# PSUM as one tile of eight banks, handed out singly, and inverse 2 copied bank by bank

## The chip, the cores and the metric

The kernel runs on one core of one Trainium2 chip. The metric is the device time of one execution in microseconds (us); of several executions the median counts. Engines are called as in the profile: PE (TensorE, matrix products into PSUM), DVE (VectorE), ACT (ScalarE), POOL (GpSimd) and SP (SyncE, which issues most DMAs here). PSUM is the memory that PE writes its results to; in this kernel it is 128 partitions by eight banks of 512 fp32 numbers.

## The reference

Two branches work on an input of 2048 positions by 640 channels, and a gate mixes them.

```python
g = sigmoid((u * gate_w).sum(-1, keepdims=True))
K = 2.0 * einsum("dn,dnl->dl", C, P).real          # P = exp(A*dt*pos), 640 channels x 128 states
y = irfft(rfft(u_t, 2*L) * rfft(K, 2*L))[:, :, :L]   # a long convolution per channel
a = y.transpose + u * D_skip
b = relu(x @ w1) @ w2                                # 640 -> 1728 -> 640
out = g * a + (1 - g) * b
```

Gate, convolution and feed-forward all take the same input: `x` is `A_u` (`u` in the convolution), so `B_x` is not used.

## The kernel before

**Feed-forward.** `feed_forward` splits the 1728 hidden units in three passes (`PARTS` 5, 5, 4 blocks of 128). Each fp32 operand is split into a high and a low part, and three products make one: in the profile `xx` holds the inputs (high and low), `w1h`, `w1l`, `w2h`, `w2l` the weights, `hh`, `hl` the hidden values (later passes keep some of these in other tiles' places, so that `w1h` or `w2h` also appear as moving operands). A group of the first product is 15 matmuls of 512 columns into one bank (`hidden`, L393; `wide`, L456); ACT takes the relu of it and DVE the low part. A group of the second product (`sums`, L496) is up to 15 matmuls of 320 columns into one bank, and DVE adds it to the running sum `q`. `trans` (L336) turns the inputs on PE in the first pass. The tiles in PSUM are called pf.

**Generation of the taps.** `ssm` (L854) makes the convolution's taps K out of 128 states, 16 channels at a time: `products` (L911; PSUM tile pg, four banks) and `taps` (L990; pk, one bank). The gate's matmuls use pg too (`spread_gate`, L611), and a tile pe of one bank takes the first matmuls of the program (`spin`, L602).

**Convolution.** `conv` (L1044) works on five blocks of 128 channels. Per block: stage 1 (`stage1`, L1097) multiplies the taps (`ck`) and the inputs (`xu`) by a table `tf`, four steps of four matmuls for each, into two banks; DVE turns each result with two stream transposes into `ku`. Of a result of the taps each transpose reads one bank; of a result of the inputs each reads half of both banks. Stage 2 (`stage2`, L1138; table `tm`) has eight steps of 16 matmuls into two banks: ACT copies one half of both banks to `ku`, DVE multiplies the other half of both with that copy, once into `kx` and once into `ku`, and POOL adds and subtracts. Inverse 2 (`inv2`, L1178; table `tn`) has two halves of 64 matmuls into four banks, which ACT copies out in two copies of two banks. DVE relays them (`relay`), and inverse 1 (`inv1`, L1216; table `tw`) has two steps of four matmuls into two banks, which ACT scales by the gate. The PSUM tiles of the convolution are called pc. They come from a pool of three tiles of two adjacent banks (L1058), opened when the generation's pool (pg, pe, pk; L863) is closed; pf has a pool of two single banks throughout (L229).

**Order.** Nothing is scheduled at run time. Each step is a task in a queue of its engine (`PE.ff`, `PE.s2`, `DVE.su`, ...). The string `ORDER` names a queue by a letter at each place, and `Plan.run` takes the next task from it; what is recorded in that order is each engine's program order. So feed-forward matmuls stand between those of the generation, and later between those of the convolution. `Ring` and `Token` count the buffers: a task takes tokens and others use them, and `run` only asserts that a buffer is free. Where one engine needs another's result, or a buffer that another still reads, the framework that records the kernel adds a semaphore wait, by the regions of tiles that each instruction reads and writes. In inverse 2 the first half's matmuls stand in `PE.s2` behind the eighth step of stage 2 (`LATE` = 4), its copies in `ACT.s2`. All instructions are recorded by one helper, so every row of the profile has its line, L186 (L188 after the change): one goes by the tiles' names.

## Time and profile before

| what | us |
|---|---|
| three runs | 622.92, 621.34, 622.42; median 622.42 |
| the profiled execution, its own time | 621.33 |
| its span in the trace | 619.5 |
| busy in the span: PE, DVE, ACT, POOL | 605.9, 505.9, 376.1, 83.9 |
| mean granted clock of PE | 0.997 |

A row of a group reads: line, engine, operation, the tile written `<-` the tiles read, shapes, count, then busy us and mean ns of one, then the idle us of the engine just before these instructions and what ended most of it. A row of the waits reads: engine, tile and line of the waiting instruction `<-` what released it, then us, count and the longest. A row of the timeline begins with the time from the start of the span and the duration; a number in square brackets is the idle time ahead of it and its releaser.

### The profile page before, as it was taken

The page shows a single profiled execution, that of the slowest core. Times are in us where ns is not written, and L with a number is a line of the kernel's source. Part 1 is how long each engine was busy: PE and PEld are TensorE (multiplying, and loading weights), DVE is VectorE, ACT ScalarE, POOL GpSimd, SP SyncE. Part 2 cuts the span into 40 slices and gives each one's busy share as a digit, 9 for nine tenths or more (in the row PEclk, how much of TensorE's full clock was granted, in tenths as well). Part 3 has the DMA queues.
Part 4 walks back from the last instruction along what each step waited for, and adds up shares of the span by engine and source line. Part 5 has one row for each costly group of instructions (what it writes and reads, how often), then busy time and mean ns, then how long its engine had stood idle before and what let it go on. Part 6 is the DMA issues. An engine that isn't in the chain of part 4 may idle for free.

```text
span 619.5 us, 19956 instructions
## 1 busy us (share of the span) xinstructions
PE 605.9 (98%) x8676; PEld 492.8 (80%) x8676; DVE 505.9 (82%) x841; ACT 376.1 (61%) x539; POOL 83.9 (14%) x114
## 2 busy tenths in 40 slices
PE   7999999999999999999999999999999999999997
PEld 6999998889987898898898888676646755667666
DVE  3798966899999999999999966887859768968642
ACT  3654438999999998899989821313351453432561
POOL 0000000000000000000000000024250360731735
PEclk8999999999999999999999999999999999999999
DMA  9783666135246535453643338982526766664276
GB/s 232 199 321 93 213 218 221 42 81 163 82 134 216 189 138 185 162 170 82 212 165 137 111 116 259 280 247 84 110 75 226 179 156 197 151 168 158 67 200 184
DMA packets 75457, 102.56 MB, mean 166 GB/s; under 512 B 7529, under 2 KB 58601, under 8 KB 75114
## 3 DMA queue, kind: packets, MB, share of 16 engines
q1 hardware_dynamic: 74970, 100.39, 53.8%
q8 instruction: 68, 1.11, 0.8%
q10 hardware_dynamic: 400, 0.90, 0.5%
q14 instruction: 19, 0.16, 0.1%
HBM read 62.21 MB, written 39.06 MB: 163 GB/s over the span
## 4 chain that ended last, share of the span: by engine, by line
PE 76%; ACT 8%; DVE 7%; DMA 4%; issue 2%; SPq 1%; POOL 1%; ACTq 0%; DVEq 0%; POOLq 0%
PE pf L186 51%; PE pc L186 15%; PE pk L186 6%; PE pg L186 4%; ACT sc L186 4%; DVE ku L186 3%; ACT L186 2%; SPq L186 1%; ACT mg L186 1%; DMA xu<-in_A_u_dram 1%; DMA ck<-kd 1%; DVE sc L186 1%; DVE mg L186 1%; DVE G L186 1%; DMA out_dram<-yo 1%
## 5 line engine op out<-in xcount | busy, mean ns | idle before, releaser
L186 PE MATMUL pf<-xx,w1h 128*128 128x256 f32 (+1 forms) x760 | 187.0, 344 | 0.0
L186 PEld LDWEIGHTS pf<-xx,w1h 128*128 128x128 f32 x760 | 124.9, 192 | 28.0 <-issue 13.4
L186 POOL TENSOR_TENSOR ku<-ku,kx 128x256 f32<-128x256 f32 x80 | 56.7, 738 | 473.5 <-DVE ku L186 438.3
L186 PE MATMUL pf<-xx,w1l 128*128 128x512 f32 (+1 forms) x340 | 115.9, 341 | 0.0
L186 ACT COPY ku<-pc 128x512 f32<-128x512 f32 (+1 forms) x60 | 43.7, 753 | 100.4 <-PE pc L186 89.1
L186 PE MATMUL pf<-w2h,hh 128*128 128x320 f32 x288 | 91.4, 322 | 0.3 <-DVE q L186 0.3
L186 DVE STREAM_TRANSPOSE ku<-pc 128x512 f32<-128x512 f32 x80 | 76.8, 1063 | 17.3 <-PE pc L186 17.3
L186 PE MATMUL pf<-w2l,hh 128*128 128x320 f32 x288 | 87.7, 308 | 0.0
L186 PE MATMUL pf<-w2h,hl 128*128 128x320 f32 x256 | 73.7, 313 | 0.0
L186 PEld LDWEIGHTS pf<-xx,w1l 128*128 128x128 f32 x340 | 64.9, 191 | 7.5
L186 PEld LDWEIGHTS pf<-w2h,hh 128*128 128x128 f32 x288 | 54.0, 188 | 11.1 <-issue 5.3
L186 ACT ACT_TABLE_LOAD x42 | 53.9, 1283 | 1.7 <-DVE sc L186 1.0
L186 PEld LDWEIGHTS pf<-w2l,hh 128*128 128x128 f32 x288 | 54.1, 188 | 0.2
L186 DVE TENSOR_TENSOR mg<-mg,sc 128x1024 f32<-128x1024 f32 x40 | 49.0, 1224 | 3.5 <-DVE G L186 0.5
L186 ACT COPY sc<-pg 128x1024 f32<-128x1024 f32 x40 | 40.4, 1010 | 14.7 <-PE pg L186 14.6
L186 DVE TENSOR_TENSOR sc<-sc,mg 128x1024 f32<-128x1024 f32 x40 | 48.6, 1216 | 0.0
L186 PEld LDWEIGHTS pf<-w2h,hl 128*128 128x128 f32 x256 | 46.4, 188 | 2.0 <-issue 1.2
L186 ACT ACTIVATE sc<-sc,half_pi 128x1024 f32<-128x1024 f32 x40 | 45.6, 1140 | 0.0
L186 ACT ACTIVATE hh<-pf 128x512 fp32r<-128x512 f32 (+1 forms) x40 | 20.4, 510 | 36.5 <-PE pf L186 36.5
L186 ACT ACTIVATE sc<-sc 128x1024 f32<-128x1024 f32 x40 | 42.2, 1054 | 0.2
L186 ACT ACTIVATE mg<-pg 128x1024 f32<-128x1024 f32 x40 | 41.7, 1043 | 0.2
L186 PE MATMUL pc<-ku,tm 64*32 64x256 f32 x1280 | 39.8, 379 | 0.6 <-DVE ku L186 0.5
(171 smaller groups left out, 1127.3 us busy)
## 6 DMA issues: line engine op xcount, KB each, us to landing
xx<-xt SPq DMA_DIRECT2D x24, 640.0 KB, 6.5
xt<-xx SPq DMA_DIRECT2D x16, 640.0 KB, 5.0
part<-q SPq DMA_DIRECT2D x16, 640.0 KB, 4.7
q<-part SPq DMA_DIRECT2D x16, 640.0 KB, 4.6
ws<-in_B_w_dram SPq DMA_DIRECT2D x20, 320.0 KB, 3.4
kd<-kt SPq DMA_DIRECT2D x80, 64.0 KB, 3.1
ck<-kd SPq DMA_DIRECT2D x40, 128.0 KB, 3.4
xu<-in_A_u_dram SPq DMA_DIRECT2D x10, 512.0 KB, 8.4
```

Of the source, the lines that this page charges most:

```text
L186: return lambda *a, **k: self._tc.keep_in_program_order(f(*a, **k))
```

## The change

PSUM becomes one tile `ps` of eight banks that lives throughout, and one ring `bk` hands out its banks. A `Ring` now keeps a list of free numbers; `run` gives a token the first of the list, and puts the number at its end when the last user is done. Feed-forward groups, turns of the inputs, `taps`, `spin` take one token each; `products` works in banks 0 to 3, which four tokens (`hold`) keep until the task that opens the convolution. Stage 1, stage 2 and inverse 1 take two tokens each, inverse 2 four. The two banks of a stage are no longer adjacent: stage 1 of the inputs and stage 2 address them as one strided access from the lower to the upper bank (`lo:hi + 1:hi - lo`), in the matmuls and in what reads them. Stage 1 of the taps and inverse 1 read each bank by itself. Inverse 2 is copied out by four copies of one bank per half instead of two of two banks; its matmuls and copies stand in queues of their own, `PE.s3` and `ACT.s3` (`LATE` is gone). The convolution's tables wait for a task `room` of their own, which opens the SBUF pool `cv` behind the feed-forward tasks that it names. `trans` and `spin` depend on the task that takes the held banks. `EVAC` and `EV2` are switches for other ways to copy stages 1 and 2 out (`S1` belongs to them); at 0, as set here, they add nothing. `QUEUES` and `ORDER` are new throughout.

```diff
-LATE = 4
+S1 = 2
+EVAC = dict(k=0, u=0)
+EV2 = 0
...
-    'C,N:R4,C,Ca,Cam,am,lmlAElACA3C2lCACA2amcCmC2amClmClA2CAl2CAaCamClmCAlU2CaACamCmB2CaBCB:CBCa;2C.CaQtftC2tC2tC'
+    '!PD;T4;mD;Da;DFan;aB;mDcBm2nDBDmDmBDBD2anDnD2anDmnDmDBDBm2DBaDanDmnDBmW2DaBDanDnC2DaCDC!DCDa?2D!DufuD2uD2uav'
...
 class Ring:
     def __init__(self, n):
-        self.free = n
+        self.free = list(range(n))
...
                 for b in t.take:
-                    b.ring.free -= 1
-                    assert b.ring.free >= 0, (k, n)
+                    b.slot = b.ring.free.pop(0)
                 t.fn()
                 t.done = True
                 for b in (*t.take, *t.use):
                     b.left -= 1
-                    b.ring.free += b.left == 0
+                    if b.left == 0:
+                        b.ring.free.append(b.slot)
...
-        self.pb = ctx.enter_context(tc.tile_pool(name="psf", bufs=2, space=PSUM))
+        self.ps = ctx.enter_context(tc.tile_pool(name="ps", bufs=1, space=PSUM)).tile([128, 8, 512], F32, name="ps")
...
-                        st['hb'] = st['hb', i] = pb.tile([128, 2, 256], F32, name="pf")
+                        st['hb'] = st['hb', i] = self.ps[:, b_.slot].rearrange("p (k t) -> p k t", t=256)
...
-        self.prm0 = A('PY', 'open', lambda: None)
+        self.hold = [tok('bk') for _ in range(4)]
+        self.prm0 = A('PY', 'open', lambda: None, take=self.hold)
...
-                p = self.psg.tile([128, 8, 256], F32, name="pg").rearrange("p (r x) n -> p r (x n)", x=2)
+                p = self.ps[:, :4]
...
-        opened = self.opened = A('PY', 'open', start, [self.kd_out])
+        opened = A('PY', 'open', lambda: None, [self.kd_out], use=self.hold)
+        room = self.room = A('PY', 'open', start, [opened])
...
         def stage1(kind, i, q, src):
...
-            b_ = tok('psc')
+            bs = tok('bk'), tok('bk')
...
-                p = st['p1', kind, i, q] = self.psc.tile([128, 2, 512], F32, name="pc")
+                lo, hi = sorted(b.slot for b in bs)
+                p = st['p1', kind, i, q] = self.ps[:, lo:hi + 1:hi - lo]
...
         def stage2(i, j, dep):
-            b_, x_ = tok('psc'), tok('kx')
+            bs, x_ = [tok('bk') for _ in range(2)], tok('kx')
...
-                ps = self.psc.tile([128, 2, 4, C], F32, name="pc")
+                lo, hi = sorted(b.slot for b in bs)
+                ps = self.ps[:, lo:hi + 1:hi - lo].rearrange("q p (x c) -> q p x c", c=C)
...
         def inv2(i, h, dep):
-            bs = tok('psc'), tok('psc')
+            bs = [tok('bk') for _ in range(4)]
...
-            def back(k):
+            def back(m):
                 def go():
-                    S.copy(st['X', i][:, 16 * h:16 * h + 16].rearrange("q (g m) e f -> q m g e f", m=4)[:, 2 * k:2 * k + 2],
-                           st['p3', i, h][k].rearrange("q m g (e f) -> q m g e f", f=2))
+                    S.copy(st['X', i][:, 16 * h:16 * h + 16].rearrange("q (g m) e f -> q m g e f", m=4)[:, m],
+                           self.ps[:, bs[m].slot].rearrange("q (g e f) -> q g e f", g=4, f=2))
                 return go
...
-            return vs, [A('ACT', 's2', back(k), [v], use=[bs[k], K[i]]) for k in range(2)]
+            return vs, [A('ACT', 's3', back(m), [v, *used[i]], use=[bs[m], K[i]]) for m in range(4)]
...
                 self.plan.put(fs[j][0], 'PE', 's2')
-                if j == 3 + LATE:
-                    [self.plan.put(x, 'PE', 's2') for x in iv[0][0]]
-            [self.plan.put(x, 'PE', 's2') for x in iv[1][0]]
+            [self.plan.put(x, 'PE', 's3') for y in iv for x in y[0]]
```

The order of the instructions, at two places. The first is the start of the convolution, stage 1 of the first block, on PE; names as in the kernel, `_49` and the like are the semaphores' numbers. Before:

```order
L186 MATMUL pc<-xu,tf 64x512 [waits DMAHW2_49,PE_49]
L186 MATMUL pc<-xu,tf 64x512 [waits DMAHW3_49]
L186 MATMUL pc<-xu,tf 64x512 x2
L186 MATMUL pc<-ck,tf 64x512 [waits DMAHW6_49,DVE_49,PE_49]
L186 MATMUL pc<-ck,tf 64x512 [waits DMAHW7_49]
L186 MATMUL pc<-ck,tf 64x512 x2
L186 MATMUL pf<-w2h_5601,hh_5646 128x320 [waits Activation_49]
L186 MATMUL pf<-w2l_5602,hh_5646 128x320
```

After, from the third step of the inputs on:

```order
L188 MATMUL ps<-xu,tf 64x512 [waits DVE_49] x2
L188 MATMUL ps<-xu,tf 64x512 x2
L188 MATMUL ps<-xx,w1h_5162 128x512 [waits DVE_49]
L188 MATMUL ps<-xx,w1h_5162 128x512
L188 MATMUL ps<-xx,w1l_5163 128x512
L188 MATMUL ps<-xx,w1h_5162 128x512 [waits DVE_49]
L188 MATMUL ps<-xx,w1h_5162 128x512
L188 MATMUL ps<-xx,w1l_5163 128x512
L188 MATMUL ps<-w2h_5387,hh_5458 128x320 [waits DVE_49,Activation_49]
L188 MATMUL ps<-w2l_5388,hh_5458 128x320
```

Pieces of three matmuls of a feed-forward group now stand behind a step of the inputs, and the first matmul of each piece waits for DVE. On DVE the transposes of these results stand like this; before:

```order
L186 STREAM_TRANSPOSE ku<-pc 128x16x32 [waits PE_49]
L186 TENSOR_TENSOR w2l_5602<-ws,w2h_5601 128x640 [waits DMAHW7_49,Activation_49]
L186 SCALAR_TENSOR_TENSOR hl_5647<-pf,hh_5646 128x512 [waits Activation_49]
L186 STREAM_TRANSPOSE ku<-pc 128x16x32
L186 STREAM_TRANSPOSE ku<-pc 128x16x32 [waits PE_49]
```

After:

```order
L188 STREAM_TRANSPOSE ku<-ps 128x16x32 x2
L188 STREAM_TRANSPOSE ku<-ps 128x16x32 [waits PE_49] x5
L188 TENSOR_TENSOR w2l_5453<-ws,w2h_5452 128x640 [waits DMAHW4_49,Activation_49]
L188 STREAM_TRANSPOSE ku<-ps 128x16x32 [waits PE_49] x3
L188 SCALAR_TENSOR_TENSOR hl_5459<-ps,hh_5458 128x512 [waits Activation_49]
```

Before, the first transpose of a result waits for PE and the second doesn't; now each of several in a row waits for PE by itself. The second place is stage 2 of the third block on PE: 16 matmuls of a step (`tm`), and a feed-forward group of 15 behind it, of which the first six are shown before, and all after. Before:

```order
L186 MATMUL pc<-ku,tm 32x256 [waits DVE_49,PE_49]
L186 MATMUL pc<-ku,tm 32x256 x15
L186 MATMUL pf<-xx,w1h_5372 128x512 [waits DVE_49]
L186 MATMUL pf<-xx,w1h_5372 128x512
L186 MATMUL pf<-xx,w1l_5373 128x512
L186 MATMUL pf<-xx,w1h_5372 128x512 x2
L186 MATMUL pf<-xx,w1l_5373 128x512
```

After:

```order
L188 MATMUL ps<-ku,tm 32x256 x16
L188 MATMUL ps<-xx,w1h_5162 128x512 [waits DVE_49]
L188 MATMUL ps<-xx,w1h_5162 128x512
L188 MATMUL ps<-xx,w1l_5163 128x512
L188 MATMUL ps<-xx,w1h_5162 128x512 x2
L188 MATMUL ps<-xx,w1l_5163 128x512
L188 MATMUL ps<-xx,w1h_5162 128x512 [waits Activation_49]
L188 MATMUL ps<-xx,w1h_5162 128x512
L188 MATMUL ps<-xx,w1l_5163 128x512
L188 MATMUL ps<-xx,w1h_5162 128x512 [waits DVE_49]
L188 MATMUL ps<-xx,w1h_5162 128x512
L188 MATMUL ps<-xx,w1l_5163 128x512
```

In this excerpt the group goes to bank 4, and the results of stage 2 that ACT and DVE read lie in banks 2 and 5. Before, a feed-forward group waits at its first matmul only; now also at the seventh and the tenth.

## The prediction

> **What bounds the kernel now.** I read the page first, for the engines' shares.

> ```profile
> span 619.5 us, 19956 instructions
> PE 605.9 (98%) x8676; PEld 492.8 (80%) x8676; DVE 505.9 (82%) x841; ACT 376.1 (61%) x539; POOL 83.9 (14%) x114
> ```

> TensorE has 13.6 us of idle time in the span. The table by stretches says where: start, generation of the taps (124 to 341), convolution (368 to 589), end.

> ```profile
> core 0: us, PE busy (x) PEld busy (x) DVE busy (x) ACT busy (x) POOL busy (x), PEclk, DMA share, GB/s
> 0.00:31.00 31.00, 26.25 (x171) 25.02 (x172) 16.95 (x41) 15.41 (x29) 0.88 (x7) 0.94 0.83 216
> 124.00:341.00 217.00, 216.08 (x3625) 189.81 (x3624) 209.29 (x358) 198.76 (x220) 0.00 (x0) 1.00 0.47 151
> 368.00:589.00 221.00, 219.22 (x3497) 145.38 (x3498) 169.13 (x239) 75.98 (x145) 70.43 (x95) 1.00 0.59 166
> 589.00:619.50 30.50, 26.30 (x147) 20.53 (x147) 10.63 (x19) 12.58 (x32) 12.55 (x13) 1.00 0.73 194
> ```

> So TensorE bounds every stage: it idles 0.9 us in the generation and 1.8 us in the convolution, and the rest lies in start and end. The waits of the convolution say the same: the other engines wait for TensorE, and TensorE hardly for them.

> ```profile
> ACT ku L186 <- PE pc L186: 89.1, 42, 15.2
> DVE ku L186 <- PE pc L186: 17.3, 9, 6.4
> PEld pc L186 <- ACT ku L186: 6.4, 15, 0.8
> ```

> Whatever makes TensorE wait there is paid in full; whatever frees the other engines saves nothing.

> **What the change can save.** TensorE's instructions are the same 5904 matmuls. (a) Idle time: at most 0.9 + 1.8 us; I take 1.0. (b) Changes of kind: the order has 267 changes between kinds of matmul, now 246; from feed-forward to another kind 105, now 89. A round trip costs this:

> ```profile
> 378.25 0.31 PE L186 MATMUL pf<-w2h,gw 128*128 128x320 f32 x1
> 378.49 1.95 PE L186 MATMUL pc<-ck,tf 64*64 64x512 f32 x16
> 380.36 0.73 PE L186 MATMUL pf<-xx,w1h 128*128 128x512 f32 x2
> 380.94 0.39 PE L186 MATMUL pf<-xx,w1l 128*128 128x512 f32 x1
> ...
> 383.89 0.62 PE L186 MATMUL pf<-xx,w1h 128*128 128x512 f32 x2
> 384.35 0.39 PE L186 MATMUL pf<-xx,w1l 128*128 128x512 f32 x1
> ```

> Going in, 0.24 us from start to start instead of 0.147 (the next rows show that slot: 604.17 follows 604.02 in steps of 0.147); coming back, 0.58 instead of 0.46 for two. That is 0.21 us, 16 times: 3.4 us saved. (c) The start: the gate's matmul no longer shares banks with the first transposes, so this wait of 1.68 us goes:

> ```profile
> 9.25 0.41 DVE L186 TENSOR_TENSOR xx<-pg,xx 128x256 fp32r<-128x256 f32 x1
> 9.72 1.34 PE L186 MATMUL pg<-gw,ones 1*128 1x512 f32 x4 [1.68 <-DVE xx L186]
> 12.35 1.56 DVE L186 TENSOR_TENSOR w1l<-wq,w1h 128x640 fp32r<-128x640 f32 x2 [0.81 <-ACT w1h L186]
> ```

> but one subtraction of the weights (1.56 / 2 = 0.78 us, after its cast) is now queued ahead of the two subtractions that the first feed-forward matmuls wait for. Between a saving of 1.7 and a loss of 0.8 I take a saving of 0.7. (d) Inverse 2: 40 copies of one bank for 20 of two. By the copies' rows below that is 40 x 0.590 - 20 x 1.079 = 2.0 us more on ScalarE, which is busy 76 of 221 us: nothing. Its queue of its own, the held banks and the later opening of the tables are only order. Together the savings are 5.1 us.

> **What the change adds.** Before, the two banks of a convolution result were one tile, side by side. Now stage 1 of u and stage 2 take two free banks wherever they lie, and read both with one strided access: banks 3 and 7, say. All of PSUM is one tile, and the waits of the built program treat such a read as covering every bank from the first to the last. In the first excerpt of the change the three feed-forward matmuls go to bank 6 and the transposes read banks 3 and 7, and nothing else is shared; yet the transpose waits for the matmul ahead of it, and the next matmul waits for the transpose. Following the list of free banks through the order and the semaphore counts through the program, I find 57 two-bank reads that wait for a matmul into a bank between theirs, and 52 matmuls that wait for such a read: behind a u transpose 18, behind a stage-2 multiply 24, behind a stage-2 copy alone 10. All lie in the convolution. Before, there were none. Queued behind each such matmul is everything on TensorE.

> The price of one, where the read itself waits for the matmul just ahead (so that neither engine can get ahead of it): the tail of that matmul until the reader starts, the reader, and the hop back. The tail and the hop:

> ```profile
> 367.38 0.31 PE L186 MATMUL pf<-w2h,gw 128*128 128x320 f32 x1
> 367.53 0.31 PE L186 MATMUL pf<-w2h,hh 128*128 128x320 f32 x1
> ...
> 367.73 0.49 DVE L186 TENSOR_TENSOR q<-pf,q 128x320 f32<-128x320 f32 x1 [1.71 <-PE pf L186]
> ...
> 604.02 0.31 PE L186 MATMUL pf<-w2l,w2h 128*128 128x320 f32 x1
> 604.17 0.31 PE L186 MATMUL pf<-w2h,w2l 128*128 128x320 f32 x1
> 604.21 1.01 DVE L186 SCALAR_TENSOR_TENSOR q<-pf,omg,q 128x320 f32<-128x320 f32 x2 [4.78 <-POOL q L186]
> 604.82 0.42 PE L186 MATMUL pf<-w2h,hh 128*128 128x320 f32 x1 [0.34 <-DVE q L186]
> ```

> The group that ends with the matmul of 367.38 releases VectorE at 367.73, 0.20 us after TensorE's next slot (367.53). The first of the two operations at 604.21 ends at about 604.74, and TensorE goes on at 604.82: 0.08 us. The readers:

> ```profile
> L186 DVE STREAM_TRANSPOSE ku<-pc 128x512 f32<-128x512 f32 x80 | 76.8, 1063 | 17.3 <-PE pc L186 17.3
> L186 DVE TENSOR_TENSOR kx<-pc,ku 128x512 f32<-128x512 f32 x40 | 27.2, 680 | 4.8 <-ACT ku L186 4.3 <-POOL ku L186 0.6
> L186 ACT COPY ku<-pc 128x512 f32<-128x512 f32 x40 | 23.6, 590 | 51.7 <-PE pc L186 40.4 <-issue 11.1
> L186 ACT COPY ku<-pc 128x1024 f32<-128x1024 f32 x20 | 20.4, 1079 | 48.7 <-PE pc L186 48.7
> ```

> So 1.34 us behind a transpose (1.06 + 0.28), 0.96 behind a multiply, 0.87 behind a copy. For each of the 52 I went back along the waits and the reader's own queue to the matmul that releases it, added these durations, and took off the matmuls that stand between, and what an earlier wait had already paid:
> - at the full price: 8 transposes (10.7), 5 multiplies (4.8), 4 copies (3.5): 19.0 us;
> - behind two or more readers in a row: 2 (4.4), 6 (11.1), 3 (5.3): 20.8 us; at one reader's price it would be 11.1;
> - partly covered by matmuls between: 15 of them, 10.5 us;
> - covered: 9, nothing.

> That is 50.3 us. Apart from these, five matmuls of the convolution now take a bank right behind its true reader, with nothing between: 4.2 us (one 1.53, two 0.96, the rest small).

> TensorE's clock comes on top.

> ```profile
> 8.00:12.00 4.00, 2.33 (x12) 1.68 (x12) 3.49 (x6) 2.79 (x7) 0.00 (x0) 0.97 1.10 287
> 12.00:16.00 4.00, 4.00 (x25) 4.00 (x23) 1.56 (x2) 1.16 (x3) 0.00 (x0) 0.60 1.02 262
> ```

> After a stretch in which TensorE was busy 2.33 of 4 us, the granted clock fell to 0.60 in the next: 0.40 x 4 + 0.03 x 4 = 1.7 us of work lost. The new waits stand densely at the changes from one block of 128 channels to the next; I count two such drops, 3.4 us, between none and ten (17 us). [...]

> The sum, against the profiled execution's 621.3 us: 621.3 + 50.3 + 4.2 + 3.4 - 5.1 = 674.1. That execution is 1.1 us below the median of 622.4, so 675.

> **Rivals.**
> - The waits are met already, and only the savings are left: 622.4 - 5.1 = 617, or no change where the new order saves less. For it: VectorE is busy 169 of 221 us there and ScalarE 76, so a reader could be done before TensorE comes. [...] Against it: 17 of the 52 pairs are closed on both sides, and no idle time of VectorE opens them. It decides only if under five pairs bind. Chance 0.06 (faster 0.04, the same 0.02).
> - Only the closed pairs bind, since every pause lets the readers catch up for the others: 622.4 + 19.0 - 5.1 = 636, to 646 with the chains at one reader's price. For it: 52 us of VectorE's idle time in the stretch. Chance 0.08.
> - The pauses pull the clock down again and again, or delay VectorE so that true dependencies come late: ten drops and nothing covered (8 + 5 + 4 and the others at full price 55.9, chains 9.7 more): above 704. Chance 0.10.

> **The numbers.** Forecast 675, chance 0.76. Its own range is 646 (the 19.0, the chains at one price, 11.1, less 6) to 704 (55.9 + 9.7 + 4.2 + 17 - 5.1 above 622.4). To 640, half of the second rival is held as well, and 8 in 10 with it: 640 to 704. A measurement of this kernel can tell about 0.3% (1.9 us) from no change; every case but the first is slower by far more: faster 0.04, same 0.02, slower 0.94.

> **What would show it.** In the profile after: TensorE's busy share falls to about 92% and all of its new idle time lies in the convolution; the waits list TensorE behind VectorE's ku and kx and ScalarE's ku some 40 times at about 1 us; timelines there show a transpose between two matmuls of one feed-forward group. Start, generation and end keep their lengths within 3 us. I am wrong if the convolution keeps 221 us, if TensorE's waits there are for Pool or DMA, or if the loss lies in the generation.

## The result

The changed kernel takes 691.75 us (median of four runs, 690.3 to 695.63) against 621.88 us before: 1.114 times as long (95% interval 1.108 to 1.119), 70 us more. The profiled execution took 692.34 us. Of the four executions of experiment e2 below one took 762.8 us, at a mean granted clock of 0.741 against 0.976 to 0.979 in the other three, and its numbers leave that one out. The page of the changed kernel:

```profile
span 690.5 us, 19975 instructions
...
PE 629.0 (91%) x8676; PEld 503.5 (73%) x8676; DVE 509.9 (74%) x841; ACT 377.1 (55%) x559; POOL 83.9 (12%) x114
...
PE   7999999999999999999999998577887896699897
...
PEclk9999999999999999999999989679999899699999
```

TensorE's busy time has grown by 23.1 us and its idle time from 13.6 to 61.5 us, by 47.9; together that is the 71.0 us by which the span grew. The other engines' busy time has hardly changed. In the two rows of 40 slices (17.3 us each) the clock first falls in the 24th and idle time first shows in the 25th, some 25 us into the convolution, and both go on to its end. The stages, start to end:

```profile
core 0: us, PE busy (x) PEld busy (x) DVE busy (x) ACT busy (x) POOL busy (x), PEclk, DMA share, GB/s
0.00:31.00 31.00, 27.25 (x187) 25.72 (x188) 20.16 (x49) 15.96 (x30) 0.87 (x7) 1.00 0.91 242
...
124.00:341.00 217.00, 214.79 (x3606) 189.47 (x3605) 207.32 (x351) 198.30 (x216) 0.00 (x0) 1.00 0.45 148
...
372.00:660.00 288.00, 238.52 (x3434) 149.06 (x3438) 171.46 (x235) 75.53 (x161) 71.09 (x95) 0.91 0.46 125
660.00:690.50 30.50, 26.03 (x177) 21.44 (x160) 10.97 (x19) 13.09 (x35) 11.90 (x13) 0.96 0.72 195
```

Start, generation and end differ from before by little: idle time is 1.0 us less at the start, 1.3 us more in the generation and 0.3 us more at the end. The convolution has 49.5 us of idle time where 1.8 us were before, and a clock of 0.91. What TensorE waits for there stands first in its list of waits (us, times, longest):

```profile
PE ps L188 <- DVE ku L188: 27.8, 29, 2.9
PE ps L188 <- DVE kx L188: 10.5, 9, 2.9
PE ps L188 <- ACT ku L188: 9.3, 8, 3.0
```

These are 46 waits of 1.03 us in the mean, all in the convolution and all for the three readers of two banks: by the operation that releases TensorE, 17 (17.2 us) are for a transpose, 21 (21.2 us) for a multiply (12 of them stand in the row of `ku` beside the transposes) and 8 (9.3 us) for a copy. The list does not tell a false wait from a true hand-over, of a bank that a reader still holds; the prediction counted five of those. The readers themselves are no slower on banks that lie apart (before: 1063, 680 and 590 ns; the row of the copies now also holds the 40 one-bank copies of inverse 2, and e7, with adjacent banks, has 608 ns for it):

```profile
L188 DVE STREAM_TRANSPOSE ku<-ps 128x512 f32<-128x512 f32 x80 | 77.3, 1057 | 33.3 <-PE ps L188 32.2 <-ACT ku L188 0.7 <-ACT yo L188 0.5
L188 DVE TENSOR_TENSOR kx<-ps,ku 128x512 f32<-128x512 f32 x40 | 27.4, 685 | 33.2 <-ACT ku L188 22.4 <-PE ps L188 9.2 <-POOL ku L188 0.9
L188 ACT COPY ku<-ps 128x512 f32<-128x512 f32 x80 | 44.7, 603 | 157.9 <-PE ps L188 138.7 <-DVE ku L188 11.8 <-DVE kx L188 7.2
```

The timeline at the first place of the order (stage 1 of the inputs, and the feed-forward group cut in pieces of three matmuls) shows the hand-over in both directions. The numbers are start, duration, and in brackets the idle time ahead and its releaser:

```profile
392.96 2.29 PE L188 MATMUL ps<-xu,tf 64*64 64x512 f32 x16
393.56 1.08 DVE L188 STREAM_TRANSPOSE ku<-ps 128x512 f32<-128x512 f32 x1 [1.52 <-PE ps L188]
395.30 1.04 DVE L188 STREAM_TRANSPOSE ku<-ps 128x512 f32<-128x512 f32 x1 [0.65 <-PE ps L188]
396.39 0.73 PE L188 MATMUL ps<-xx,w1h 128*128 128x512 f32 x2 [1.14 <-DVE ku L188]
396.96 0.39 PE L188 MATMUL ps<-xx,w1l 128*128 128x512 f32 x1
397.39 1.92 DVE L188 STREAM_TRANSPOSE ku<-ps 128x512 f32<-128x512 f32 x2 [1.05 <-PE ps L188]
398.48 1.22 PE L188 MATMUL ps<-xx,w1h 128*128 128x512 f32 x2 [1.13 <-DVE ku L188]
```

A transpose runs from 395.30 to 396.34, TensorE waits 1.14 us and starts at 396.39; its three matmuls end at 397.35, VectorE has waited 1.05 us and starts at 397.39; TensorE waits again, 1.13 us. The two engines take turns, though they share no bank.

The clock, in stretches cut at its steps:

```profile
395.20:398.20 3.00, 1.01 (x6) 0.48 (x3) 1.85 (x2) 0.00 (x0) 0.00 (x0) 0.97 0.85 325
398.20:405.00 6.80, 6.34 (x23) 2.83 (x23) 3.62 (x5) 2.75 (x4) 0.00 (x0) 0.51 0.01 3
405.00:412.00 7.00, 6.82 (x47) 5.90 (x48) 5.80 (x9) 0.00 (x0) 0.00 (x0) 1.00 0.91 158
431.50:435.40 3.90, 1.40 (x65) 0.99 (x58) 1.53 (x3) 1.04 (x2) 0.17 (x2) 1.00 0.00 0
435.40:456.10 20.70, 14.34 (x225) 6.69 (x226) 5.36 (x7) 4.25 (x8) 2.75 (x4) 0.51 0.01 2
```

After 3 us with TensorE busy for a third of them it works at half clock for 6.8 us; at the change to the second block it stays there for 20.5 us, while the pauses go on. There are seven such stretches in the convolution. Summed over pieces of 0.5 us (busy time times what is missing from the clock) they cost 21.8 us of work; before, the one stretch at the start cost 1.7.

So the 71.0 us are 47.9 of idle time, 20.1 of clock, and 3.0 of other busy time. The first and the last term are taken apart by the experiments.

### The profile page after: what moved, and what is told of

It reads as the page before. It is cut to its first block, busy times and chain, and to the rows that moved or that the text cites. A ratio compares the mean times of both kernels' runs of the same rounds, so it can differ in the third digit from the quotient of the medians.

```text
span 690.5 us, 19975 instructions
## 1 busy us (share of the span) xinstructions
PE 629.0 (91%) x8676; PEld 503.5 (73%) x8676; DVE 509.9 (74%) x841; ACT 377.1 (55%) x559; POOL 83.9 (12%) x114
## 4 chain that ended last, share of the span: by engine, by line
PE 75%; DVE 13%; ACT 6%; issue 2%; DMA 2%; SPq 1%; POOL 0%; DVEq 0%; ACTq 0%; POOLq 0%
PE ps L188 75%; DVE ku L188 7%; DVE kx L188 2%; ACT ku L188 2%; ACT sc L188 2%; DMA xu<-in_A_u_dram 1%; ACT L188 1%; SPq L188 1%; DVE hl L188 1%; DMA tf<-in_t_f_dram 1%; DVE sc L188 1%; ACT mg L188 1%; DMA ps<-hl 0%; DVE G L188 0%; DVE xu L188 0%
## 5 line engine op out<-in xcount | busy, mean ns | idle before, releaser
L188 PE MATMUL ps<-xx,w1h 128*128 128x256 f32 (+1 forms) x760 | 188.8, 346 | 15.8 <-DVE ku L188 8.7
L188 PEld LDWEIGHTS ps<-xx,w1h 128*128 128x128 f32 x760 | 125.4, 192 | 45.0 <-DVE ku L188 13.4
L188 PE MATMUL ps<-xx,w1l 128*128 128x512 f32 (+1 forms) x340 | 116.7, 343 | 0.0
L188 DVE STREAM_TRANSPOSE ku<-ps 128x512 f32<-128x512 f32 x80 | 77.3, 1057 | 33.3 <-PE ps L188 32.2
L188 PE MATMUL ps<-w2h,hh 128*128 128x320 f32 x288 | 91.5, 322 | 2.2 <-DVE ku L188 1.0
L188 PE MATMUL ps<-w2l,hh 128*128 128x320 f32 x288 | 88.8, 312 | 0.0
L188 PE MATMUL ps<-w2h,hl 128*128 128x320 f32 x256 | 73.5, 313 | 0.0
L188 PEld LDWEIGHTS ps<-xx,w1l 128*128 128x128 f32 x340 | 65.3, 192 | 7.8
L188 PEld LDWEIGHTS ps<-w2h,hh 128*128 128x128 f32 x288 | 54.7, 190 | 9.2 <-issue 3.0
L188 PEld LDWEIGHTS ps<-w2l,hh 128*128 128x128 f32 x288 | 54.8, 190 | 1.1 <-issue 0.6
L188 DVE TENSOR_TENSOR sc<-sc,mg 128x1024 f32<-128x1024 f32 x40 | 48.7, 1218 | 0.0
L188 PEld LDWEIGHTS ps<-ku,tm 64*32 64x32 f32 x1280 | 24.1, 107 | 25.7 <-ACT ku L188 6.8
```

The costliest lines, as they stand in the source:

```text
L188: return lambda *a, **k: self._tc.keep_in_program_order(f(*a, **k))
```

## The experiments

The theory (A): the two-bank accesses over banks that lie apart, which the program takes for everything between, make the waits; the fallen clock follows from the pauses. The rivals: (B) the new order, the queues of inverse 2 or true hand-overs of banks; (C) waits as in A, but the clock from the new order of matmuls. "My sum" is the sum over all stalls as the prediction made it, by the same durations, applied to each kernel's order: 58.1 us for the changed kernel.

**e1: adjacent banks.** Only the choice of the free bank is changed; a token that stage 1 of the inputs or stage 2 takes is marked `pair`.

```diff
+                pair = [b for b in t.take if b.pair]
+                if pair:
+                    free = pair[0].ring.free
+                    age = {x: a for a, x in enumerate(free)}
+                    lo = min((x for x in free if x + 1 in age), key=lambda x: (max(age[x], age[x + 1]), x), default=None)
...
+                        for x in (lo, lo + 1):
+                            free.remove(x)
+                            free.insert(x - lo, x)
                 for b in t.take:
                     b.slot = b.ring.free.pop(0)
```

> The changed kernel with one difference: stage 1 of the inputs and stage 2 take two banks that lie side by side when two such are free. Order, copies and work are the same. By the built program 6 false waits of TensorE are left of 52. Theory A (the false waits are the loss, and the fallen clock is their consequence): the 58 us that my sum gives for the changed kernel become 9, the granted clock goes back to at least 0.99, and the time is about 622 (616 to 632). Rival B (the new order, the queues of inverse 2 or true hand-overs of banks make TensorE wait): 680 to 695. Rival C (the waits go, but the lower clock of 0.96 comes from the new order of matmuls): 640 to 650 with a clock below 0.98.

Measured: 620.57 us (617.56 to 622.0), 0.9971 of before (0.9955 to 0.9986). The page and the convolution's stretch:

```profile
span 618.3 us, 20013 instructions
...
PE 602.0 (97%) x8676; PEld 494.6 (80%) x8676; DVE 507.3 (82%) x841; ACT 376.4 (61%) x559; POOL 84.0 (14%) x114
```

```profile
372.00:590.00 218.00, 213.10 (x3461) 141.57 (x3460) 169.05 (x236) 76.86 (x164) 71.16 (x95) 1.00 0.60 167
```

Here is the same place of the order again, with the same pieces of the feed-forward group:

```profile
393.94 3.72 DVE L199 STREAM_TRANSPOSE ku<-ps 128x512 f32<-128x512 f32 x4 [0.71 <-PE ps L199]
...
395.03 1.09 PE L199 MATMUL ps<-xu,tf 64*64 64x512 f32 x8 [0.27 <-DVE ku L199]
396.05 0.73 PE L199 MATMUL ps<-xx,w1h 128*128 128x512 f32 x2
396.62 0.39 PE L199 MATMUL ps<-xx,w1l 128*128 128x512 f32 x1
396.85 0.62 PE L199 MATMUL ps<-xx,w1h 128*128 128x512 f32 x2
```

VectorE makes its four transposes in one piece and TensorE runs the group beside them. What is left of TensorE's waits for the three readers, in the whole span:

```profile
PE ps L199 <- ACT ku L199: 1.4, 2, 0.7
PE ps L199 <- DVE ku L199: 1.1, 2, 0.9
PE ps L199 <- DVE kx L199: 0.9, 1, 0.9
```

With order, queues, copies and work unchanged, all of the loss is gone, waits and clock. C falls, and so does B as far as order and queues go. e1 also deals the banks out differently, so the five true hand-overs (4.2 us by the prediction) may have gone with the false waits; e5 and e6, in the order before, bear on that.

**e2 and e3: one class of readers each.** The marks are set in stage 1 of the inputs alone (e2) or in stage 2 alone (e3).

> As e1, but only stage 1 of the inputs takes adjacent banks; stage 2 takes what comes. 19 false waits are left, my sum gives 29.7 us of stalls instead of 58 (changed kernel) and 9 (e1). Theory A, with the clock's loss in proportion to the stalls (23 us for 49): 622 + 20.7 + 9.7 = about 652. Rival B: 680 to 695. Rival C: 664.

> As e1, but only stage 2 takes adjacent banks; stage 1 of the inputs takes what comes. 23 false waits are left, 27.1 us by my sum. Theory A: 622 + 18.1 + 8.5 = about 649. Rival B: 680 to 695. Rival C: 661.

Measured: e2 652.02 us (1.048 of before, 1.045 to 1.051), e3 646.42 us (1.040, 1.037 to 1.042); expected 652 and 649. The first fix alone leaves about a half of the loss by waits and the second about a third (24.8 and 18.7 us of 52.1, by the table below).

**e4: the order before, banks apart.** The kernel before, with PSUM as one tile and fixed places:

```diff
+PF, PAIRS = [3, 4], [(0, 5), (1, 6), (2, 7)]
...
-                p = st['p1', kind, i, q] = self.psc.tile([128, 2, 512], F32, name="pc")
+                p = st['p1', kind, i, q] = self.pair()
...
+    def pair(self):
+        lo, hi = self.bank('pc')
+        return self.ps[:, lo:hi + 1:hi - lo]
```

> The kernel before, with its own order and its own copies, and PSUM as one tile: in the convolution the feed-forward groups rotate over banks 3 and 4, and the two-bank results over the pairs 0 and 5, 1 and 6, 2 and 7, each read as one strided access. Nothing else differs from before. The built program has 128 false waits of TensorE and my sum gives 160 us. Theory A: 622 + 155 = 777 without any loss of clock, up to 850 with a loss in the changed kernel's proportion. Rival B (order and queues are the cause): 622.

Measured: 874.01 us (1.406; 1.400 to 1.412). `bank` hands the places out in turn, so a result that is still to be read can be overwritten: some results of this kernel are computed from wrong data, while the instructions are the same. The mechanism shows in the old order too; the loss is above the upper end that I gave (850). e5 repeats it with a list of free places.

**e5 and e6: all pairs apart, and one of three.** In e5 a place is taken from a list of the free ones, in e6 the places differ as well:

```diff
-PF, PAIRS = [3, 4], [(0, 5), (1, 6), (2, 7)]
+PF, PAIRS = [3, 4], [(0, 1), (2, 5), (6, 7)]
```

> As e4 (the kernel before with its own order, feed-forward in banks 3 and 4, two-bank results in 0 and 5, 1 and 6, 2 and 7), but the banks come from a list of free ones instead of in turn, so that no live result is overwritten. My sum gives 161 us of stalls where the kernel before has 6. Theory A: 622 + 155 of waits + some 92 of lost clock, as in e4: 870. Rival B (waits between banks that are not shared cost nothing): 622.

> As e5, but only one pair of the three encloses the feed-forward banks (2 and 5 around 3 and 4; the others are 0 and 1, 6 and 7). 37 false waits of TensorE instead of 127, my sum gives 31.6 us. Theory A1 (lost clock goes with the waits, 0.42 us for each us of waiting as in the changed kernel): 622 + 25.7 + 10.8 = 658. Theory A2 (the clock falls only where pauses stand densely, and here they are spread): 648 with a clock of 0.99 or more. Rival B: 622.

Measured: e5 869.22 us (1.397; 1.392 to 1.403), e6 652.94 us (1.049; 1.045 to 1.052). The page and the first waits of e5:

```profile
span 865.9 us, 19910 instructions
...
PE 716.8 (83%) x8676; PEld 530.5 (61%) x8676; DVE 514.6 (59%) x841; ACT 375.8 (43%) x539; POOL 83.7 (10%) x114
...
PEclk8999999999999999999675575887569656987589
```

```profile
PE ps L187 <- DVE ku L187: 69.8, 65, 2.2
PE ps L187 <- DVE kx L187: 38.6, 28, 2.9
PE ps L187 <- ACT ku L187: 27.1, 25, 2.3
```

And of e6:

```profile
span 650.6 us, 19956 instructions
...
PE 613.5 (94%) x8676; PEld 493.0 (76%) x8676; DVE 509.1 (78%) x841; ACT 375.3 (58%) x539; POOL 83.6 (13%) x114
```

```profile
PE ps L187 <- DVE ku L187: 15.4, 20, 1.2
PE ps L187 <- ACT ku L187: 5.7, 7, 1.1
PE ps L187 <- DVE kx L187: 3.5, 4, 0.9
```

With the old order, the old copies and the old queues, PSUM as one tile with one pair or all three apart makes the kernel 30 or 246 us slower than before (623.02 us, run beside them); between e5 and e6 nothing differs but the numbers of the banks. The old order with all pairs adjacent in one tile was not run. For e5 the lost clock in the expectation (92 us) was taken from e4, so its agreement bears on the waits and not on a reckoning of the clock. e6 lies between A1 (658) and A2 (648): the waits cost 2 us more than summed, and the lost clock is 3.2 us above before's, half of it from one fall in the convolution and half from a longer one at the start.

**e7: the copies of inverse 2, alone.**

```diff
-                    S.copy(st['X', i][:, 16 * h:16 * h + 16].rearrange("q (g m) e f -> q m g e f", m=4)[:, 2 * k:2 * k + 2],
-                           st['p3', i, h][k].rearrange("q m g (e f) -> q m g e f", f=2))
+                    for m in (2 * k, 2 * k + 1):
+                        S.copy(st['X', i][:, 16 * h:16 * h + 16].rearrange("q (g m) e f -> q m g e f", m=4)[:, m],
+                               st['p3', i, h][k][:, m % 2].rearrange("q g (e f) -> q g e f", f=2))
```

> The kernel before with one difference: each copy of inverse 2 (two banks) is two copies of one bank, in the same place of the order. By the rows 0.590 x 2 - 1.079 = 0.10 us more per copy, 2.0 us in all on ScalarE. Forecast: nothing on the time, 622 (620.5 to 623.5). Rival: the relay behind the copies is late for each half, 0.2 us ten times, and TensorE has nothing else to do: 624.

Measured: 622.65 us, 0.9993 of before (0.9975 to 1.0012): nothing, as forecast. With 40 copies of one bank in the place of 20 of two, the copies of stage 2 and inverse 2 together take 44.6 us of ScalarE (before 23.6 + 20.4 = 44.0); the expectation had 2.0 us more.

```profile
L186 ACT COPY ku<-pc 128x512 f32<-128x512 f32 x80 | 44.6, 608 | 104.9 <-PE pc L186 87.5 <-issue 11.6 <-DVE ku L186 5.7
```

**e8: another choice of free banks.** As e1, and a step that needs one bank takes the second of the free ones at drawn places:

```diff
-                    b.slot = b.ring.free.pop(0)
+                    free = b.ring.free
+                    if b.ring is self.rings.get('bk') and not b.pair and self.rings.get('psx') is None and len(free) > 1 and RNG.random() < 0.3:
+                        free.insert(0, free.pop(1))
+                    b.slot = free.pop(0)
```

> As e1 (adjacent banks for stage 1 of the inputs and stage 2), but a step that needs one bank takes the second oldest of the free ones instead of the oldest at places that a fixed draw names; of two dozen draws this one leaves the least by my sum, 6.0 us of stalls where e1 has 9.0. If the sum holds at this size: 617.6. Rival (below some 5 us it says nothing): as e1, 620.6.

Measured: 619.2 us, 0.9944 of before (0.9924 to 0.9964). It is the fastest of the runs, by 0.6% against before; it lies between its two expectations (617.6 and 620.6), and the intervals of e1 and e8 overlap, so whether a sum of stalls holds at 3 us stays open.

## Why the prediction was right, and where its sum was off

The spans can be taken apart in the same way for all kernels: idle time of TensorE (span less busy), work lost to the clock (summed over pieces of 0.5 us), and the rest of the busy time.

| kernel | span | idle | lost clock | other busy |
|---|---|---|---|---|
| before | 619.5 | 13.6 | 1.7 | 604.2 |
| changed | 690.5 | 61.5 | 21.8 | 607.2 |
| e1 | 618.3 | 16.3 | 1.7 | 600.3 |
| e2 | 652.3 | 33.5 | 10.9 | 607.9 |
| e3 | 643.5 | 31.6 | 8.2 | 603.7 |
| e5 | 865.9 | 149.1 | 94.5 | 622.3 |
| e6 | 650.6 | 37.1 | 4.9 | 608.6 |

A wait shows in two columns. Most of it is idle time; its tail, the duration of the last matmul ahead of a pause beyond its slot, counts as busy (the one at 396.96 above has 0.39 us, and in e1 the next starts 0.23 us after it, at 396.85 behind 396.62). I put down to tails that "other busy" is 6.9 us larger in the changed kernel than in e1 with the same matmuls in the same order. That is argued and not shown: it is 0.15 us for each of 46 waits, but in e2 the same difference is 7.6 us for 20 waits.

- **The waits: right, and the size too.** Forecast 50.3 + 4.2 = 54.5 us, in 52 waits less 9 that are covered, and five true ones. Measured: 46 waits; 47.9 us of idle time more than before, and 6.9 of "other busy" more than e1, 54.8. That it fits within 0.3 us is partly luck, as the idle time also holds the small changes at the start and in the generation, and the hop back, priced at 0.08 us from an end taken as 604.74, was 0.05 (that operation ends at 604.76). Against e1, where my sum leaves 9.0 of 58.1, it is 45.2 + 6.9 = 52.1 for 49.1. The other kernels bear the sum out: e5 135.5 + 18.1 = 153.6 for 155, e6 23.5 + 4.4 = 27.9 for 25.7, e3 (against e1) 15.3 + 3.4 = 18.7 for 18.1, e2 17.2 + 7.6 = 24.8 for 20.7.
- **The savings: right for the changes of kind, not for the idle time.** Forecast 3.4 us for 16 round trips fewer. e1 has the changed order without the false waits, and its other busy time is 604.2 - 600.3 = 3.9 us less than before (e8, with the same order, 601.4: 2.8 less). The 1.0 us of idle time that I took off in generation and convolution was not saved: e1 idles 2.0 and 4.9 us in those stretches instead of 0.9 and 1.8. In the convolution most of it are the few waits left (3.4 us); in the generation 1.7 us are pauses for which the profile shows no releaser. The 0.7 us at the start came: 31 - 27.25 = 3.75 us of idle time there, 4.75 before.
- **The clock: the step that was off.** "I count two such drops, 3.4 us, between none and ten (17 us)": it was 20.1 us more than before, above the end that I gave. Of the 18.2 us by which the span grew beyond the forecast (71.0 against 54.5 + 3.4 - 5.1 = 52.8), 16.7 are this term, 1.2 are savings that did not come, and 0.3 waits. Both factors failed. No run shows a count of two, or the ten of the upper end, which were my estimates; there were seven stretches of half clock. And 1.7 us each is only the shortest: at half clock TensorE stayed for 3.4, 6.8 or 20.5 us, and each of the 67 intervals of half clock with a busy share below 0.82 was followed by another (table in the last section). The third rival, which named repeated drops, had this term right; but its other half (nothing covered, above 704) did not come. The result still lies in the range, whose upper end held 17 us of clock and all 52 waits at full price.
- **The rivals.** The first (waits met already) and the second (only the closed pairs bind) are out by 46 waits of about 1 us. In e1, with the two banks adjacent, the engines work in different banks side by side and hardly wait: five waits of TensorE for the three readers, 3.4 us, instead of 46. Whether a read of banks that lie apart could run without the wait on those between was not tried; that would have taken away the wait alone.
- **The signs named ahead.** Busy share 91% (said: about 92%), nearly all new idle time in the convolution (47.7 us; the generation has 1.3 more), some 40 waits for the three readers (46), a transpose between two matmuls of one group: as said. The convolution begins 4.0 us later than before (372.2 instead of 368.2), beyond the 3 us that I gave; in e1 it begins later still (373.4) at a shorter total, so this is no loss: the new order puts 51 more feed-forward matmuls ahead of it (1783 instead of 1732, in both kernels).

The inverse's copies bank by bank cost nothing (e7), as forecast. Which of the pauses bring the clock down was seen, not tried by itself: in the convolutions looked at (changed, e2, e3, e5, e6) TensorE had been busy 0.20 to 0.58 of the 3.4 us ahead of each fall. No run here moved pauses together or apart at the same sum and the same order; e6 and e3 come near it.

## What to carry to other kernels

A strided access over banks (or slots) that lie apart was taken by the program here as everything between, and banks in between that another engine was working on became waits in both directions (46 of TensorE, 1.03 us in the mean): hand out such buffers side by side, and look for the waits in the built program before a run, since they can be counted and priced there from a profile of the old kernel. Waits of about 1 us on the bound engine cost more than their sum in the changed kernel: 20.1 us of clock came on top of 47.9 us of idle time. Reckon the clock by the stretches of 3.4 us in which the engine is busy less than half of the time (26 of 28 such here were followed by half clock), and by how long its share at half clock stays below 0.82 (all 67 such here were followed by another), not by a few single drops. When an allocator and an order change together, changing the allocator alone (e1) tells which of them the loss belongs to.

## What the runs showed of the hardware

| clock in the interval | TensorE busy | intervals | next interval at half clock |
|---|---|---|---|
| 1.0 | below 0.5 | 28 | 26 |
| 1.0 | 0.5 to 0.6 | 20 | 3 |
| 1.0 | above 0.6 | 298 | 0 |
| 0.5 | below 0.82 | 67 | 67 |
| 0.5 | above 0.82 | 36 | 7 |

So one interval with TensorE busy for less than half of it was nearly always followed by half clock, in 26 of 28 cases. At half clock all 67 intervals with a share below 0.82 were followed by another; matmuls took longer there (eight of stage 1 of the inputs 1.99 us at 442.10 in the changed kernel, 1.09 us at 395.03 in e1). A share between 0.6 and 0.82, with which the full clock never fell (above 0.6: none of 298), did not bring it back. In the changed kernel and e5 the clock went to and fro between half and full in this way, with seven and 17 falls in the convolution, and 20.1 and 92.8 us of lost clock more than before.

The sum of the pauses alone does not give the lost clock: e6 has 23.5 us of idle time more than before and lost 1.7 us of clock in the convolution, e3 has 15.3 us more than e1 and lost 6.5. In e6 no interval had a share below 0.5, and the one fall came behind a share of 0.53; in e3 a share of 0.34 was followed by 17.1 us of half clock. In e6 the one fall is seen in this table of stretches of 25 us, and TensorE is busy 83 to 100% of each:

```profile
368.00:393.00 25.00, 25.00 (x156) 18.70 (x155) 13.38 (x18) 2.55 (x4) 0.00 (x0) 1.00 0.80 221
...
493.00:518.00 25.00, 20.85 (x441) 14.54 (x442) 15.28 (x25) 8.70 (x18) 8.30 (x12) 1.00 0.63 152
...
568.00:593.00 25.00, 21.83 (x287) 13.35 (x294) 16.82 (x20) 5.50 (x12) 2.07 (x3) 0.93 0.50 140
```
